# A gated mix of full and local attention: other PSUM banks for the last K block and the first Q, a second DMA queue for the last output rows, and new planner numbers

## The chip, the core and the metric

The kernel runs on one core of one Trainium2 chip. The core has five engines with their own instruction streams: TensorE (PE in the profile; its weight loads are shown apart as PEld), VectorE (DVE), ScalarE (ACT), GpSimd (POOL) and SyncE (SP, which issues nearly all DMAs here). The metric is device time in microseconds, the median of several runs. PSUM, into which TensorE writes, has eight banks of 512 fp32 columns on 128 partitions.

## What is computed

Two attentions over the same 2048 tokens of 640 channels, 32 heads of 20 channels each, mixed by a gate for each token. Branch A is full attention; branch B looks at eight earlier tokens, two apart. In the reference (cut):

```python
def _A_ref(x, wqkv, wo):
    q, k, v = ...                                  # 32 heads of 20
    scores = jnp.einsum("bhqd,bhkd->bhqk", q, k) * scale
    p = _softmax(scores, axis=-1)
    o = jnp.einsum("bhqk,bhkd->bhqd", p, v)
    return merge_heads(o) @ wo

def _B_ref(x, wqkv, wo):
    W, dil = 8, 2
    idx = pos[:, None] - (jnp.arange(W) * dil)[None, :]   # masked where < 0
    ...                                            # softmax over the 8 taps
    return merge_heads(o) @ wo

g = _sigmoid((x * gate_w).sum(-1, keepdims=True))
return g * _A_ref(x, A_wqkv, A_wo) + (1 - g) * _B_ref(x, B_wqkv, B_wo)
```

## The kernel before

**Units and tiles.** Branch A is cut into 32 groups, one for each of 4 query chunks of 512 tokens and 8 quads of heads. A group has 16 K blocks of 128 keys times 4 heads: 64 score blocks of 128 x 512, 2048 in all. TensorE makes a score block as `kT` times `qT` (L1508), an exponential turns it into weights, and TensorE multiplies these by `vA` into the output bank `obank` (L1576). The exponential of most blocks runs on ACT (L1531), two blocks (128x1024) or three (128x1536) to an instruction: a tile. The others "ride": a fourth row group of TensorE makes them into a spare bank, and DVE forms the exponential as an integer that is read as bf16 (L1521, then three shifted copies at L797 that go through `obank` with weighted V). A column of ones in `vA` gives the softmax sum.

**PSUM.** `score[0]` and `score[1]` have three banks each, which alternate from tile to tile; `obank` and `side0` have one each. The third bank of each score tensor, when a tile has only two blocks, serves as a side bank: `side[0]` is `side0`, `side[1]` the third bank of `score[0]`, `side[2]` that of `score[1]`. All other TensorE work (projections, branch B, output projection; L558) and the rides use side banks.

**The order of the work.** The Python code is a list scheduler. `_Sched.task` keeps a modelled time for each engine and appends each task to the stream of its engine; `emit` writes the five streams with semaphores. So the order on each engine is fixed when the program is built. For each tile `s` the main loop issues the score matmuls, the exponential, perhaps a multiplication by V, and then lets other work in (`spend`, `run_side`) until the modelled end of the previous exponential plus a slack. Where modelled TensorE load is below a bound (`FILL`), `filler` (L1597) puts in matmuls whose result is not used. `PLAN` (L50 to L102) sets 18 numbers of these rules anew at certain tiles: slacks, priorities, due times, the bound of the filler, when a DVE ride may open.

**The head** (L1287 to L1345) stands before that loop, in an order written out by hand. x arrives in four chunks, `turn` transposes each into a score tensor (chunks 0 and 2 into `score[0]`, 1 and 3 into `score[1]`; 1280 fp32 columns, so into the third bank too), and `x_out` copies it to `xT` on ACT and DVE. `k_first(0)` to `k_first(3)` project the K of the first head quad, 512 keys each, alternating between `side0` and `obank` (`kbank`, L1252); `k_max` (DVE) takes the largest absolute value in each row, and `k_out` (ACT) copies the block to `kT`. At L1314 the first Q block is projected into `side[1]`. DVE combines the maxima to `KM[0]`, takes |Q| into `qabs[0]`, TensorE adds `KM[0]` times `qabs[0]` to the same bank (L1326; a bound on the scores, which stands in for the row maximum), and DVE scales the bank into `qT[0]` (L1331), which the first scores need. `v_first` and `v_out` make the first V block in `side0`. `bank_free` and `obank_first` tell the scheduler when the banks come free.

**The tail** (L1048 to L1085) makes the last 512 output rows, in four blocks of 128. When the last group's output is normalised (`gen_norm`, DVE), five matmul groups (L1057) add its share; what the other heads and branch B give lies ready in SBUF (`pre`) for blocks 0 and 1, and in two side banks for blocks 2 and 3 (`gen_prefold2`, L1036). ACT copies the first 512 columns of blocks 2 and 3 to `tout` (L1076), DVE adds blocks 0 and 1 (L1079) and the last 128 columns of all four (`tout_r`, L1070). Then SP issues four DMAs of 160 KB each, in the order 0, 1, 2, 3 (L1084).

```python
    kbank = lambda tcc: (side[0], ("side", 0)) if tcc % 2 == 0 else (obank, "obank")   # L1252
...
        for blk in range(4):                                                         # L1082
            row = (QCN - 1) * 512 + blk * P
            T("sp", 2.0, lambda e, blk=blk, row=row: e.dma_start(out_v[row:row + P, :], tout[blk]),
              reads=[("tout", blk), "tout_r"], writes=[("out", row)], dma=True)
```

Of the kernel before, what the change touches and what calls it, by code (L numbers as in the profile page):

```python
# [50 lines left out]
    0: ((0.36, 0.81), 0.32, 2.5, 6.6, 0.49, -1.0, -0.1, 11.8, 7.0, 7.2, 0.52, 0.47, 4.4, 4.44, 0.0, 0.85, 2, 0.0),  # L51
    10: ((0.41, 0.67), 0.29, 2.5, 6.6, 0.49, -1.0, -0.32, 10.6, 6.7, 7.2, 0.52, 0.61, 4.4, 4.44, 0.0, 0.85, 2, 0.0),
    30: ((0.3, 0.64), 0.32, 2.5, 2.5, 0.49, -1.0, -0.1, 11.8, 7.0, 6.95, 0.47, 0.5, 4.97, 4.0, 0.0, 0.85, 2, 0.0),
    40: ((0.42, 0.67), 0.29, 2.5, 6.6, 0.49, -1.0, -0.32, 10.6, 6.7, 7.2, 0.52, 0.61, 4.4, 4.44, 0.0, 0.85, 2, 0),
    70: ((0.41, 0.67), 0.29, 2.5, 2.5, 0.83, -1.02, -0.32, 10.6, 5.5, 7.2, 0.42, 0.61, 5.71, 4.44, -0.04, 0.85, 3, 0.0),
    80: ((0.42, 0.67), 0.29, 5.5, 6.6, 0.49, -1.0, -0.32, 10.6, 6.7, 7.2, 0.52, 0.48, 4.4, 4.44, 0.12, 0.85, 2, 0),
    90: ((0.42, 0.67), 0.05, 2.5, 6.6, 0.49, -1.0, -0.32, 10.6, 6.7, 7.2, 0.52, 0.61, 4.4, 4.44, 0.0, 0.6, 2, 0),
    110: ((0.3, 0.64), 0.32, 2.5, 1.0, 0.49, -1.0, -0.1, 11.8, 7.0, 7.2, 0.4, 0.47, 4.77, 3.55, -0.02, 0.85, 2, 0.0),
    120: ((0.3, 0.61), 0.32, 2.5, 6.3, 0.49, -1.0, -0.1, 10.63, 7.0, 7.2, 0.4, 0.56, 4.29, 4.0, 0.0, 0.85, 2, 1),
    130: ((0.3, 0.61), 0.28, 2.5, 6.3, 0.62, -1.0, -0.1, 10.63, 7.0, 7.2, 0.39, 0.56, 4.29, 4.0, 0.0, 0.85, 2, -3),  # L60
    140: ((0.3, 0.61), 0.22, 2.5, 5.5, 0.4, -1.0, 0.01, 9.77, 7.0, 7.2, 0.33, 0.21, 4.29, 4.0, 0.0, 0.85, 2, 0.0),
    150: ((0.3, 0.64), 0.32, 2.5, 2.5, 0.49, -1.0, -0.35, 11.8, 7.0, 7.2, 0.52, 0.47, 4.4, 4.0, 0.1, 0.85, 2, 0.0),
    190: ((0.3, 0.64), 0.32, 1.0, 2.5, 0.49, -1.0, -0.1, 11.8, 7.0, 7.2, 0.55, 0.47, 4.56, 4.0, 0.0, 0.85, 2, 0.0),
    200: ((0.3, 0.64), 0.32, 1.0, 2.5, 0.49, -0.57, 0.17, 11.8, 7.0, 7.2, 0.55, 0.47, 4.56, 4.0, 0.04, 0.85, 2, 0.0),
    210: ((0.3, 0.64), 0.32, 2.5, 2.5, 0.49, 0.26, 0.1, 11.8, 4.5, 11.1, 0.56, 0.32, 4.97, 4.0, -0.25, 0.85, 2, -3),
    230: ((0.3, 0.64), 0.32, 2.5, 2.5, 0.49, 0.05, -0.54, 11.8, 6.7, 11.1, 0.56, 0.47, 5.29, 2.82, -0.48, 0.85, 2, -3),
    240: ((0.3, 0.64), 0.32, 1.0, 6.3, 0.49, -0.85, -0.1, 11.39, 6.7, 11.1, 0.56, 0.27, 4.97, 4.0, -0.25, 0.85, 2, -3),
    260: ((0.3, 0.64), 0.32, 1.0, 6.3, 0.49, -0.34, -0.1, 11.39, 6.7, 10.86, 0.56, 0.27, 4.97, 4.0, 0.08, 0.85, 2, -3),
    290: ((0.3, 0.64), 0.32, 1.0, 6.3, 0.49, -0.34, -0.1, 11.39, 4.5, 10.86, 0.56, 0.27, 4.97, 4.0, 0.08, 0.85, 2, -3),
    300: ((0.3, 0.64), 0.32, 1.0, 6.3, 0.49, -0.34, -0.1, 11.39, 4.5, 10.86, 0.56, 0.27, 6.29, 4.0, 0.05, 0.85, 2, -3),  # L70
    320: ((0.3, 0.64), 0.27, 1.0, 6.3, 0.49, -0.83, -0.1, 11.39, 4.5, 10.86, 0.69, 0.23, 5.37, 4.0, 0.05, 0.61, 2, -3),
    330: ((0.3, 0.64), 0.27, 1.0, 6.3, 0.49, -0.72, -0.1, 11.39, 4.5, 7.69, 0.69, 0.23, 5.37, 4.0, 0.05, 0.61, 2, -3),
    340: ((0.3, 0.64), 0.14, 1.0, 6.3, 0.49, -1.05, 0.17, 11.39, 6.7, 10.63, 0.3, 0.34, 5.37, 4.43, 0.05, 0.61, 2, -3),
    350: ((0.3, 0.64), 0.16, 1.0, 6.3, 0.49, -0.25, -0.1, 8.61, 6.7, 10.86, 0.56, 0.27, 4.97, 4.0, 0.08, 0.85, 2, -3),
    360: ((0.3, 0.64), 0.27, 1.0, 5.5, 0.7, -0.83, -0.1, 12.93, 4.5, 11.67, 0.69, 0.23, 5.37, 4.0, 0.05, 0.61, 2, -3),
    390: ((0.3, 0.64), 0.27, 1.0, 6.3, 0.7, -0.83, -0.1, 12.93, 7.0, 10.86, 0.69, 0.23, 5.37, 4.0, 0.2, 0.61, 2, -3),
    400: ((0.3, 0.64), 0.27, 1.0, 6.3, 0.7, -0.83, -0.1, 12.93, 7.0, 9.69, 0.69, 0.23, 5.37, 1.85, 0.2, 0.6, 2, -3),
    420: ((0.3, 0.64), 0.27, 1.0, 6.3, 0.7, -0.83, -0.07, 12.93, 4.5, 10.86, 0.5, 0.23, 5.37, 4.0, 0.1, 0.61, 2, -3),
    430: ((0.3, 0.64), 0.27, 1.0, 6.3, 0.7, -0.83, -0.07, 12.93, 6.2, 10.86, 0.5, 0.23, 5.37, 4.0, 0.1, 0.61, 2, -3),
    440: ((0.3, 0.64), 0.27, 1.0, 6.3, 0.7, -0.83, -0.07, 12.93, 4.5, 10.86, 0.5, 0.23, 5.64, 4.45, 0.1, 0.75, 2, -3),  # L80
    460: ((0.3, 0.64), 0.27, 1.0, 5.5, 0.8, -0.83, -0.07, 11.24, 4.5, 10.15, 0.5, 0.23, 5.12, 4.0, 0.1, 0.61, 2, -3),
    470: ((0.3, 0.62), 0.27, 1.0, 5.5, 0.8, -0.83, -0.03, 11.24, 4.5, 10.15, 0.5, 0.23, 5.12, 4.0, 0.2, 0.61, 2, 0),
    480: ((0.3, 0.62), 0.27, 1.0, 5.5, 0.8, -0.83, -0.03, 11.24, 4.5, 10.15, 0.5, 0.2, 5.12, 4.0, 0.2, 0.63, 2, 0),
    490: ((0.3, 0.64), 0.27, 1.0, 5.5, 0.16, -1.11, -0.07, 11.24, 4.5, 10.15, 0.5, 0.22, 5.12, 4.0, 0.1, 0.61, 2, -3),
# [1686 lines left out]
```

## Time and profile before

| what | value |
|---|---|
| median of 5 runs | 841.44 us (840.33 to 842.42) |
| the profiled execution, device time | 840.33 us |
| its span, first to last instruction | 838.5 us |
| granted TensorE clock | 0.998 of full |
| ACT busy, share of the span | 808.3 us, 96% |
| DVE busy | 675.8 us, 81% |
| DMA | 29.16 MB, 35 GB/s on average |

The span is 1.8 us shorter than the device time of the same execution; what lies around it is launch and end. The five runs lie within 2.1 us, and the profiled one is the fastest of them. ACT, DVE and TensorE are all busy for most of the span, so the share of busy time alone doesn't tell which of them sets the end; the order of waits does. A row "xN" of the timeline merges N like instructions, and its second number is the time from the start of the first to the end of the last.

### The profile page before, as it was taken

The page shows a single profiled execution, that of the slowest core. Times are in us where ns is not written, and L with a number is a line of the kernel's source. Part 1 is how long each engine was busy: PE and PEld are TensorE (multiplying, and loading weights), DVE is VectorE, ACT ScalarE, POOL GpSimd, SP SyncE. Part 2 cuts the span into 40 slices and gives each one's busy share as a digit, 9 for nine tenths or more (in the row PEclk, how much of TensorE's full clock was granted, in tenths as well). Part 3 has the DMA queues.
Part 4 walks back from the last instruction along what each step waited for, and adds up shares of the span by engine and source line. Part 5 has one row for each costly group of instructions (what it writes and reads, how often), then busy time and mean ns, then how long its engine had stood idle before and what let it go on. Part 6 is the DMA issues. An engine that isn't in the chain of part 4 may idle for free.

```text
span 838.5 us, 29878 instructions
## 1 busy us (share of the span) xinstructions
PE 790.9 (94%) x12795; PEld 293.3 (35%) x12798; DVE 675.8 (81%) x1183; ACT 808.3 (96%) x747; POOL 129.7 (15%) x177
## 2 busy tenths in 40 slices
PE   8999999999999999999998898999899999999997
PEld 4332322333334333433333333333342333342223
DVE  7577787779887888787888888898898878888763
ACT  4999999999999999999999999999999999999994
POOL 5040111620110110111110111111011111102100
PEclk9999999999999999999999999999999999999999
DMA  9002121200111101010101111010010010100000
GB/s 312 30 19 46 41 45 34 70 16 18 33 29 39 28 20 23 16 32 25 26 18 26 35 20 36 12 42 23 25 32 21 22 34 22 30 7 25 18 5 34
DMA packets 45016, 29.16 MB, mean 35 GB/s; under 512 B 27204, under 2 KB 43684, under 8 KB 44884
## 3 DMA queue, kind: packets, MB, share of 16 engines
q1 hardware_dynamic: 44884, 27.25, 12.5%
q8 instruction: 101, 1.65, 0.8%
q14 instruction: 31, 0.25, 0.1%
HBM read 11.94 MB, written 2.62 MB: 17 GB/s over the span
## 4 chain that ended last, share of the span: by engine, by line
PE 43%; ACT 39%; issue 12%; DVE 4%; SPq 1%; DMA 0%; DVEq 0%; ACTq 0%
ACT ebuf L1531 39%; PE score L1508 13%; PE side L558 10%; PE obank L1576 10%; PE score L558 5%; PE obank L1597 2%; DVE uD L1521 1%; DVE eD L797 1%; PE score L1597 1%; SPq L705 1%; PE side L1597 1%; PE obank L461 1%; PE score L1224 1%; ACT eB L914 0%; PE side L885 0%
## 5 line engine op out<-in xcount | busy, mean ns | idle before, releaser
L1531 ACT ACTIVATE ebuf<-score 128x1024 bf16<-128x1024 f32 (+1 forms) x715 | 797.0, 1261 | 9.7 <-PE score L1508 7.7
L1508 PE MATMUL score<-qT,kT 32*128 32x512 bf16 x2048 | 284.4, 384 | 31.0 <-ACT ebuf L1531 22.5
L1521 DVE TENSOR_SCALAR uD<-score 128x512 int16<-128x512 f32 x311 | 210.1, 685 | 55.9 <-PE score L1508 52.3
L1508 PEld LDWEIGHTS score<-qT,kT 32*128 32x128 bf16 x2048 | 72.0, 91 | 272.7 <-ACT ebuf L1531 125.2
L797 DVE TENSOR_SCALAR eD<-uD 128x2048 int16<-128x2048 int16 (+1 forms) x234 | 161.2, 712 | 3.8 <-PE obank L1576 2.5
L1576 PE MATMUL obank<-ebuf,vA 128*21 128x512 bf16 x1737 | 159.0, 385 | 2.8 <-ACT ebuf L1531 1.4
L558 PE MATMUL side<-xT,kvw 128*32 128x256 bf16 (+1 forms) x2580 | 106.0, 282 | 2.4 <-DVE dst L662 0.9
L789 POOL TENSOR_TENSOR vS<-vA,vw 128x252 bf16<-128x252 bf16 x78 | 53.3, 688 | 275.0 <-PE obank L1576 234.4
L1576 PE MATMUL obank<-eD,vS 128*21 128x512 bf16 x933 | 81.8, 379 | 0.0
L558 PEld LDWEIGHTS side<-xT,kvw 128*32 128x32 bf16 x2580 | 60.7, 96 | 37.5 <-issue 19.9
L765 POOL TENSOR_TENSOR rcp<-rcp,gA 128x16 f32<-128x16 f32 x31 | 9.8, 315 | 368.3 <-DVE rcp L763 368.3
L1576 PEld LDWEIGHTS obank<-ebuf,vA 128*21 128x21 bf16 x1737 | 37.6, 89 | 83.2 <-issue 69.7
L970 DVE TENSOR_TENSOR stage<-qkvB,repB 128x1280 bf16<-128x1280 bf16 x64 | 52.3, 841 | 0.1
L853 DVE CAST qkvB<-side 128x512 bf16<-128x512 f32 (+1 forms) x72 | 42.2, 595 | 11.3 <-PE side L558 10.7
L869 DVE TENSOR_TENSOR stage<-qkvB 128x1280 bf16<-128x1280 bf16 x64 | 50.5, 827 | 0.2
L558 PE MATMUL side<-stage,ident 128*32 128x512 bf16 (+1 forms) x768 | 49.1, 346 | 0.7 <-DVE dst L662 0.5
L1597 PE MATMUL obank<-xT,zero 128*32 128x512 bf16 x560 | 43.6, 382 | 0.0
L770 POOL TENSOR_TENSOR oN<-oTt,rcp 128x512 bf16<-128x512 f32 x31 | 32.5, 1048 | 2.4
L759 DVE STREAM_TRANSPOSE oTt<-obank 128x512 f32<-128x512 f32 x32 | 22.8, 712 | 11.1 <-PE obank L1576 11.0
L1576 PE MATMUL obank<-uD,vA 128*21 128x512 bf16 x311 | 30.3, 379 | 0.0
L772 DVE STREAM_TRANSPOSE oN<-oN 128x512 bf16<-128x512 bf16 x32 | 22.6, 705 | 9.3 <-POOL oN L770 9.0
L1576 PEld LDWEIGHTS obank<-eD,vS 128*21 128x21 bf16 x933 | 23.0, 91 | 15.8 <-issue 2.3
(161 smaller groups left out, 575.5 us busy)
## 6 DMA issues: line engine op xcount, KB each, us to landing
repB<-eB SPq DMA_DIRECT2D x128, 32.0 KB
WqP<-in_A_wqkv_dram SPq DMA_DIRECT2D x16, 160.0 KB
stage<-in_B_wqkv_dram SPq DMA_DIRECT2D x1, 2400.0 KB
oTd<-oN SPq DMA_DIRECT2D x108, 20.0 KB
qT<-dst SPq DMA_DIRECT2D x104, 20.0 KB
out_dram<-outsb SPq DMA_DIRECT2D x12, 160.0 KB
kvw<-in_A_wqkv_dram SPq DMA_DIRECT2D x2, 800.0 KB
oTd<-in_A_x_dram SPq DMA_DIRECT2D x2, 640.0 KB
```

The source lines that it names most:

```text
L558: ins = e.matmul(o[j:k, :], l[:, j:k], r, start=(first and i == 0), stop=(last and i == n - 1), skip_group_check=True)
L770: T(en, c2, lambda e: e.tensor_tensor(oo, ii, ib, ALU.mult), reads=["rcp", "oTt"], writes=["oN0"])
L789: T("pool", 0.7, lambda e: e.tensor_tensor(vS[:, d % 2, :, :], _ap(vA, (kb * NQ + q) * 4 * DV, [[0, K - 1], [1, 4 * DV]]), _ap(vw, 0, [[1, ...
L797: T("dve", 0.11 + 0.1334 * n, lambda e, k=k, sl=sl: e.tensor_scalar(eD[:, sl % NS, 0:512 * n].bitcast(I16), uD[d % 2][:, 0:512 * n].bitcas ...
L853: t = TB(dvc(n * TOK), lambda e, o=o, i=i: e.tensor_copy(o, i), reads=[("side", b)], writes=[key])
L869: TB(dvc(CN * TOK, 2), lambda e, w=w, ks=ks: e.tensor_tensor(prodB(w), qB[:, :, :], ks, ALU.mult), reads=["qB", "kB"], writes=[("prod", w) ...
L970: TB(dvc(CN * TOK, 2), lambda e, w=w, vs=vs, rr=rr: e.tensor_tensor(prodB(w), vs, rr, ALU.mult), reads=["vB", ("repB", w4 % NR)], writes=[ ...
L1508: ins = e.matmul(o, kT[32 * j:32 * j + 32, q, kb * P:(kb + 1) * P], qT[g % NQT][32 * j:32 * j + 32, :], start=True, stop=True)
L1521: t = T("dve", 0.69, lambda e: e.tensor_scalar(uD[d % 2][:, 512 * i:512 * (i + 1)].bitcast(I16), side[x], UOFF, 0.0, op0=ALU.add, op1=ALU. ...
L1531: exps[s] = T("act", actc(512 * n), lambda e: e.activation(ebuf[s % NE][:, 0:512 * n], score[s % 2][:, 0:512 * n], ACTF.Exp, scale=LN2 / S ...
L1576: ins = e.matmul(obank[32 * j:32 * j + DV, :], v, src, start=(kb == 0), stop=(last and k >= len(lst) - 4), skip_group_check=True)
L1597: ins = e.matmul(o[32 * j:32 * j + 32, :], w[:, 32 * j:32 * j + 32] if best else w[:, :], xT[:, 0, 0:512], start=bool(best), stop=bool(bes ...
```

## The change

Four edits:

- The head's last K block (`k_first(3)`) is projected into `side[1]`, the third bank of `score[0]`, in place of `obank`, and the first Q block into `obank` in place of `side[1]`. What reads these banks (`k_max`, `k_out`, |Q|, the bound's matmul, the scaling to `qT[0]`) follows.
- The times at which the scheduler takes the banks as free follow too: `side[1]` and `side[2]` after `k_out(3)`, `obank` after the scaling to `qT[0]`.
- The last four output DMAs are issued in the order 2, 3, 0, 1: blocks 2 and 3 from ACT's queue, blocks 0 and 1 from SP's.
- All rows of `PLAN` are replaced: 46 rows in place of 51, at other tiles and with other numbers. The rules that read them stay.

```diff
 PLAN = {
-    0: ((0.36, 0.81), 0.32, 2.5, 6.6, 0.49, -1.0, -0.1, 11.8, 7.0, 7.2, 0.52, 0.47, 4.4, 4.44, 0.0, 0.85, 2, 0.0),
-    10: ((0.41, 0.67), 0.29, 2.5, 6.6, 0.49, -1.0, -0.32, 10.6, 6.7, 7.2, 0.52, 0.61, 4.4, 4.44, 0.0, 0.85, 2, 0.0),
...
-    320: ((0.3, 0.64), 0.27, 1.0, 6.3, 0.49, -0.83, -0.1, 11.39, 4.5, 10.86, 0.69, 0.23, 5.37, 4.0, 0.05, 0.61, 2, -3),
...
+    0: ((0.3, 0.64), 0.32, 2.5, 2.5, 0.49, -1.0, -0.16, 11.8, 7.0, 8.62, 0.51, 0.47, 4.21, 4.0, 0.0, 0.85, 2, 0.0),
+    8: ((0.25, 0.64), 0.27, 2.5, 2.5, 0.49, -1.0, -0.27, 12.76, 7.0, 7.2, 0.52, 0.47, 4.4, 4.0, 0.0, 0.85, 3, 0.0),
...
+    232: ((0.34, 0.66), 0.37, 2.5, 2.5, 1.29, -1.0, -0.1, 11.8, 5.5, 6.1, 0.5, 0.54, 4.4, 3.8, 0.0, 0.71, 1, -3),
...
 }
@@ tail
-        for blk in range(4):
+        for blk in (2, 3, 0, 1):
             row = (QCN - 1) * 512 + blk * P
-            T("sp", 2.0, lambda e, blk=blk, row=row: e.dma_start(out_v[row:row + P, :], tout[blk]),
+            T("act" if blk > 1 else "sp", 2.0, lambda e, blk=blk, row=row: e.dma_start(out_v[row:row + P, :], tout[blk]),
               reads=[("tout", blk), "tout_r"], writes=[("out", row)], dma=True)
@@ head
-    kbank = lambda tcc: (side[0], ("side", 0)) if tcc % 2 == 0 else (obank, "obank")
+    kbank = lambda tcc: ((side[0], ("side", 0)), (obank, "obank"), (side[0], ("side", 0)), (side[1], ("side", 1)))[tcc]
...
-    T("pe", 1.07, proj5(side[1][:, :], lambda c: WqP[:, c, :], None, 0), reads=WQ + XT(0), writes=[("side", 1)])
+    T("pe", 1.07, proj5(obank[:, :], lambda c: WqP[:, c, :], None, 0), reads=WQ + XT(0), writes=["obank"])
...
-        qabs[0][:, :].bitcast(U16), side[1][:, :].bitcast(U16)[:, 1:1024:2], 0x7FFF, None, op0=ALU.bitwise_and),
-      reads=[("side", 1)], writes=[("qabs", 0)])
-    T("pe", 0.215, lambda e: e.matmul(side[1][:, :], KM[0], qabs[0][:, :], start=False, stop=True, skip_group_check=True),
-      reads=[("KM", 0), ("qabs", 0)], accum=[("side", 1)])
+        qabs[0][:, :].bitcast(U16), obank[:, :].bitcast(U16)[:, 1:1024:2], 0x7FFF, None, op0=ALU.bitwise_and),
+      reads=["obank"], writes=[("qabs", 0)])
+    T("pe", 0.215, lambda e: e.matmul(obank[:, :], KM[0], qabs[0][:, :], start=False, stop=True, skip_group_check=True),
+      reads=[("KM", 0), ("qabs", 0)], accum=["obank"])
     v_first()
     t = k_out(3)
-    obank_first = t.end + LAT["act"]
-    t = T("dve", dvc(512), lambda e: e.tensor_scalar(qT[0][:, :], side[1][:, :], OCT, offs[:, 0:1], op0=ALU.mult, op1=ALU.add),
-          reads=[("side", 1), "offs", ("qTz", 0)], writes=[("qT", 0)])
+    bank_free[1] = bank_free[2] = t.end + LAT["act"]
+    t = T("dve", dvc(512), lambda e: e.tensor_scalar(qT[0][:, :], obank[:, :], OCT, offs[:, 0:1], op0=ALU.mult, op1=ALU.add),
+          reads=["obank", "offs", ("qTz", 0)], writes=[("qT", 0)])
     qkeys[0] = [("qT", 0)]
+    obank_first = t.end + LAT["dve"]
     v_out()
-    bank_free[:] = [t.end + LAT["dve"] + 0.5, t.end + LAT["dve"], t.end + LAT["dve"]]
+    bank_free[0] = t.end + LAT["dve"] + 0.5
```

The scheduler lays its order anew from these numbers. Counted in the two orders: exponentials on ACT 715 before (406 of 128x1024, 308 of 128x1536, one of 128x512) and 722 after (428, 293, 1); rides on DVE 311 and 312; filler matmuls 1008 and 844; the matmuls of projections, branch B and output projection are the same in number.

## The prediction

> **What bounds the kernel now.** I read four views in this order: the groups of instructions with their shapes kept apart, the timeline of the head, that of the end, and the stretches. First the groups and two pieces of ACT's timeline.
>
> ```profile
> L1531 ACT ACTIVATE ebuf<-score 128x1536 bf16<-128x1536 f32 x308 | 432.4, 1504 | 3.8 <-PE score L1508 3.0 <-ACT ebuf L1531 0.3
> L1531 ACT ACTIVATE ebuf<-score 128x1024 bf16<-128x1024 f32 x406 | 398.5, 1078 | 5.8 <-PE score L1508 4.7
> ...
> 31.42 5.61 ACT L1531 ACTIVATE ebuf<-score 128x1024 bf16<-128x1024 f32 x6 [0.29 <-PE score L1508]
> ...
> 657.24 5.49 ACT L1531 ACTIVATE ebuf<-score 128x1536 bf16<-128x1536 f32 x4
> ```
>
> ACT hardly idles before an exponential: 9.6 us in 806 us. But one instruction overlaps the end of the one before, and that hides lost time. Six of 128x1024 take 5.61 us, so start to start (5.61 - 1.08)/5 = 0.906 us; four of 128x1536 (5.49 - 1.50)/3 = 1.33 us. The shortest steps all over the trace are 0.903 and 1.330. At these, with 0.48 for each 128x512 and 0.1 for each gate tile, ACT's work from the first exponential (19.50) to the end of the last (826.17) is 782 us. It took 806.7, so some 25 us are lost where scores come a little late. Three things make the time: a head of 19.5 us, ACT's 782 plus 25, and an end of 12.3.
>
> The two halves of ACT's stretch differ:
>
> ```profile
> 19.50:425.70 406.20, 398.93 (x366) 1.00 0.13 32
> 425.70:821.70 396.00, 393.68 (x347) 1.00 0.09 24
> ```
>
> Each half holds 864 score blocks. At the shortest steps they are 389.2 and 388.4 us of ACT, so the losses are 17.0 and 7.6. I counted what TensorE is given between the score matmuls in the first kernel's order, with 0.216 us for four 512-column matmuls side by side (20 of `obank` take 1.19 us in the chain of waits, with one change of mode), less for narrower ones (0.138, 0.108 and 0.069 for 320, 256 and 128 columns), and 0.11 for each change between row and column mode (a group after a change takes 0.33, without one 0.22): 384.6 and 352.3 us. So TensorE is 4.6 us below ACT in the first half and 36.1 in the second. ACT's loss grows where TensorE has little to spare: 9.4 us of loss for 31.5 us of slack, 0.30 for each.
>
> **Head: the last K block.** The timeline of TensorE, of ACT and of DVE there:
>
> ```profile
> 14.65 1.24 PE L1247 MATMUL obank<-xT,kvw 128*128 128x512 bf16 x5 [0.70 <-ACT kT L1268]
> 15.72 1.24 PE L1247 MATMUL score<-xT,WqP 128*128 128x512 bf16 x5
> 17.75 0.39 PE L1326 MATMUL score<-qabs,eB 128*128 128x512 bf16 x1 [0.79 <-DVE qabs L1323]
> 17.98 0.84 PE L1274 MATMUL side<-kvw,xT 128*128 128x320 bf16 x5
> 19.07 0.39 PE L1508 MATMUL score<-qT,kT 32*128 32x512 bf16 x3 [0.24 <-DVE qT L1331]
> ...
> 13.82 0.68 ACT L1268 ACTIVATE kT<-obank,onesrow 128x512 bf16<-128x512 f32 x1
> ...
> 15.92 0.69 DVE L1261 TENSOR_REDUCE kmx<-obank 128x1 f32<-128x512 f32 x1 [0.72 <-PE obank L1247]
> 16.65 0.35 DVE L1321 SCALAR_TENSOR_TENSOR eB<-eB,kmx 128x128 bf16<-128x128 bf16 x1
> 17.00 0.69 DVE L1323 TENSOR_SCALAR qabs<-score 128x512 uint16<-128x512 uint16 x1
> ```
>
> TensorE waits for ACT's copy of K block 1 out of `obank`, which ends at 14.50; the block starts at 14.65. In `side[1]` nothing is left to wait for: its last reader, the copy of x chunk 2, ended on DVE at 10.71 + 0.96 = 11.67. What is late next is x chunk 3, whose ACT copy ends at 12.90 + 1.02 = 13.92; the K block before ends on TensorE near 13.95. With the 0.12 to 0.15 from an end to the next start, K block 3 starts at 14.07, 0.58 earlier. Q follows 1.07 later, at 15.14, after the copy of 14.50 that now guards it: that wait costs nothing there. Had K block 3 no gain, it would. On DVE the maximum starts at 15.34 (DVE is free at 14.90 + 0.31 = 15.21), and all after it moves by the same 0.58, since each step there is released by the one before. The longer life of Q in `obank` holds up nothing: the next writer of `obank` in both orders is a filler, at 20.76 before, and Q is read by 18.4. The new K block is read by ACT near 16.8, before the first scores at 18.5. No load bounds this: V's and K's weights are issued by 8.5 us and the head doesn't wait for them. The head gives 0.58; bounds 0 (if DVE's chain hung on something else) and 0.70 (all of the wait).
>
> **Tail.** The end of the run, chain of waits and timeline:
>
> ```profile
> 826.47 0.22 PE obank L1576 x4
> 826.68 0.50 PE side L558 x28
> 827.18 4.76 PE score L558 x80
> 831.95 0.33 PE score L1057 x4
> ...
> 832.53 1.09 ACT L1076 ACTIVATE stage<-score 128x512 bf16<-128x512 f32 x2 [6.36 <-PE score L1057]
> 833.18 0.69 DVE L1079 TENSOR_TENSOR stage<-score,dst 128x512 bf16<-128x512 f32 x1
> 833.78 0.68 DVE L1079 TENSOR_TENSOR stage<-score,qabs 128x512 bf16<-128x512 f32 x1
> 833.90 2.21 SPq L1084 DMA_DIRECT2D out_dram<-stage  x4
> ```
>
> With E for the end of the last exponential (826.17), TensorE starts the tail's matmuls at 831.88 = E + 5.71, while the normalised output is ready on DVE at 829.49. It is TensorE's remaining projection that holds the tail: after the last product with V come 28 matmuls of 128 columns and 80 of 512. In the new order eight of the 80 and the narrow ones stand before that product (while the last exponential runs), and eight PV matmuls in place of four come after E. So E + 0.12 + 0.43 + 72 x 4.76/80 (4.28) + 0.11 for the mode = E + 4.94, a gain of 0.77. The normalised output, 0.22 later than before, is at E + 3.5: still hidden.
>
> Then the DMAs. Blocks 2 and 3 are ready when ACT's copies end, at 833.13 and 833.62, but stand in SP's queue behind block 0 (ready 833.87) and block 1 (834.46). The four issues start at 833.90, 834.49, 834.97 and 835.78; SP then waits until 837.73 for the last to land. New: ACT issues blocks 2 and 3 after its two copies, near 833.70 and 834.2 (nothing is queued behind them on ACT), SP issues 0 and 1 at 833.90 and 834.5. The last issue is 1.3 us earlier. What is late next is the transfer: 0.655 MB at the 350 GB/s of this DMA's busy slices is 1.9 us; first data came 0.87 after the first issue, so from 834.57 to 836.4 or 836.6, against 837.35 before. A DMA issued by ACT is not in the trace; bounds from SP's rows: 1.5 if it costs what SP's does and the final waits overlap, 0.3 if two queues share the engines so badly that only one of the 0.33 to 0.39 us issues is saved. I take 1.1, by the nearest row, SP's own. [...]
>
> Tail together 0.77 + 1.1 = 1.87, bounds 1.0 and 2.3.
>
> **Middle: the new order.** ACT has 22 more narrow and 15 fewer wide exponentials: 22 x 0.903 - 15 x 1.330 = -0.08 us at the shortest steps; rides on DVE (312 for 311, 0.69 each) and the shifted copies (234 for 234) are equal, and DVE is 81% busy. But narrow tiles lose more: their mean step is 0.947 before another exponential, 0.044 above the shortest, that of wide ones 1.353, 0.023 above. 22 x 0.044 - 15 x 0.023 = +0.63.
>
> TensorE's share, counted as above in the new order: 378.0 us against ACT's 389.5 in the first half, 350.2 against 388.9 in the second. Slack is 11.5 and 38.7 in place of 4.6 and 36.1: 9.5 more, at 0.30 a gain of 2.85. Most of it is 41 fillers fewer (164 matmuls, 8.9 us), and a filler stands where TensorE had a gap anyway; without fillers the slack grows by only 1.0, a gain of 0.3. I take the middle, 1.6, since either count is as near. Which of the `PLAN` numbers does what, no row shows.
>
> **Sum.** -0.58 - 1.87 - 0.08 + 0.63 - 1.6 = -3.5 us. The profiled execution took 840.33, so 836.8 for it; it lies 1.1 below the median of 841.44, so the median goes to 837.9.
>
> **Rivals.** (1) The new order is worth more than counts show. For it: 17 us are lost in the first half, where scores wait for TensorE, and only 7.6 in the second with the same kind of work. If the first half gets halfway to the second, the middle gives 4.7 in place of 1.05: 834.3. Against: the first half still has the projections, and its slack stays below 12 us. (2) The middle gives back what the ends gain, +2.4: 841.4. For it: the second half's stretch from 425.7 to 492.6 goes from 8.4 us of slack to 4.5, and the scores' bank serves 12 of the 20 Q projections in place of 6. (3) Slower: DVE empties the side banks inside the score tensors too late. A score matmul then waits, and TensorE takes nothing else meanwhile. The profile has such waits for the rides (28.1 us in 60, up to 0.9 each) and other DVE reads; ACT covers most of them. With 0.5 us uncovered at 12 more places the middle costs 6, and 841.44 - 2.45 + 6 = 845.0. It decides from 8 to 9 such places, above 843.1. Against: DVE's work is equal, and the numbers of matmuls and copies are the same.
>
> That the edit does not do what it says is excluded for the banks and the queue, which stand so in the new order.
>
> **Chances.** A measurement of this kernel tells about 0.2% (1.7 us) from no change. Forecast 0.55 (its part below 839.7), rival 1 0.15, rival 2 with the forecast's weak end 0.18, rival 3 0.12. So faster 0.70, within 0.2% 0.18, slower 0.12. The forecast's own range from the bounds: head 0 to 0.70, tail 1.0 to 2.3, TensorE 0.3 to 2.85 and narrow tiles 0.63 or nothing, so 0.7 to 5.9 of gain, 835.5 to 840.7. With the rivals, leaving out the slower one and the far end of the first: 832.5 to 842.5.
>
> **What would show it.** The first exponential at 18.9 and K block 3 at 14.07, released by x chunk 3; else the head's step is wrong. The tail's first matmul at E + 4.9, the last output issue near 834.5 less the shift, the last landing 1.0 to 1.2 us earlier against the tail's start. ACT's stretch at 805.6 us or so from first exponential to last, with more of the gain in the first half. The forecast is wrong if that stretch is longer than 808 or shorter than 802.

## The result and the profile after

The changed kernel takes 844.51 us (median of 27 runs, 840.31 to 848.92) against 841.44 for the kernel before (47 runs, 840.21 to 843.59): ratio 1.0036, 95% interval 1.0026 to 1.0046. It is slower by 0.36%. The forecast was 837.9, and 844.51 lies outside its range of 835.5 to 840.7. The runs also spread over 8.6 us where those of the kernel before spread over 3.4.

The profiled execution after has a span of 840.7 us and a device time of 842.50; that of before had 838.5 and 840.33. Line numbers in the loop and the tail are lower by 4 or 5 (L1531 is now L1527). The three parts of the span, and ACT's loss as the prediction counts it (start to start of exponentials, beyond the shortest steps 0.903 and 1.330):

| part | before | after | forecast of the difference |
|---|---|---|---|
| head, to the first exponential | 19.50 | 18.88 | -0.58 |
| ACT's stretch, first exponential to the end of the last | 806.66 | 810.52 | -1.05 |
| after the last exponential | 12.36 | 11.28 | -1.87 |
| ACT's loss within the stretch | 24.9 | 28.9 | |

The head's timeline, lines that answer to those of before:

```profile
13.94 1.24 PE L1242 MATMUL score<-xT,kvw 128*128 128x512 bf16 x5
...
15.01 1.24 PE L1242 MATMUL obank<-xT,WqP 128*128 128x512 bf16 x5
15.21 0.69 DVE L1256 TENSOR_REDUCE kmx<-score 128x1 f32<-128x512 f32 x1
...
18.88 1.45 ACT L1527 ACTIVATE ebuf<-score 128x1536 bf16<-128x1536 f32 x1 [2.19 <-PE score L1504]
```

The last K block starts at 13.94, straight after x chunk 3 (forecast 14.07, before 14.65), and the first exponential at 18.88 (18.9). The end, from the same view:

```profile
829.46 0.61 PE L1572 MATMUL obank<-ebuf,vA 128*21 128x512 bf16 x8
...
834.22 0.40 PE L1052 MATMUL score<-outsb,oN 128*128 128x128 bf16 x4
...
835.55 0.85 ACTq L1079 DMA_DIRECT2D out_dram<-stage  x2
...
836.24 0.96 SPq L1079 DMA_DIRECT2D out_dram<-stage  x2
```

The last exponential ends at E = 829.40. The tail's matmuls start at E + 4.82 (forecast 4.94, before 5.71), and the last output issue comes 2.6 us after them; it was 3.9. So in this profile head and tail moved as forecast; only the last landing did not, to which we come back. What went wrong is ACT's stretch, by 4.9 us against the forecast. Its two halves, with the exponentials' busy time:

```profile
18.88:425.70 406.82, 398.84 (x374) 1.00 0.13 33
425.70:829.40 403.70, 398.76 (x349) 1.00 0.09 24
```

Added up over 60 us stretches, the loss up to 420 us is 17.0 (before 16.9), and behind it 12.0 (before 8.0). The groups show the same number of score matmuls and slightly longer idle time of ACT before exponentials: 12.6 us in place of 9.7.

One thing stands in the trace of after that before had nowhere between head and tail: a granted clock of a half. Busy time of each engine in stretches of 3.4 us at the two places (PE, PEld, DVE, ACT, POOL with their numbers of instructions, then the granted clock; the last two numbers are of DMA):

```profile
373.40:376.80 3.40, 3.40 (x77) 1.78 (x78) 2.48 (x6) 3.40 (x4) 0.61 (x1) 1.00 0.29 101
376.80:380.20 3.40, 2.57 (x29) 0.59 (x17) 3.19 (x9) 3.18 (x4) 0.00 (x0) 1.00 0.00 0
380.20:383.60 3.40, 3.38 (x53) 1.14 (x54) 2.29 (x6) 3.28 (x6) 1.83 (x3) 0.51 0.11 29
...
752.30:755.70 3.40, 2.42 (x28) 0.72 (x24) 3.05 (x6) 3.40 (x5) 0.00 (x0) 1.00 0.00 0
755.70:759.10 3.40, 3.35 (x30) 0.77 (x27) 2.03 (x8) 2.96 (x3) 1.84 (x3) 0.50 0.02 5
```

In each case a thin stretch (29 and 28 matmuls, where the one ahead of the first has 77) is followed by one at half clock, 3.41 us long in the trace's record of the clock. In the stretch at 376.8 a score matmul takes 414 ns on average, in the next one 568; a product with V 382 and 600. In both thin stretches branch B's chain of maxima runs on DVE. The timeline at 378 us, where TensorE waits:

```profile
377.72 0.10 PEld L1504 LDWEIGHTS score<-qT,kT 32*128 32x128 bf16 x3 [0.44 <-DVE uD L1517]
...
378.52 0.28 DVE L902 TENSOR_TENSOR repB<-repB 32x256 bf16<-32x256 bf16 x1
378.73 0.67 DVE L1517 TENSOR_SCALAR uD<-score 128x512 int16<-128x512 f32 x1
378.85 0.39 PE L906 MATMUL side<-repB,negRep 32*128 32x512 bf16 x1 [0.42 <-DVE repB L902]
```

No filler stands between. In 28 executions of the changed kernel span and mean granted clock go together (correlation -0.84; a fit gives 511 us for a whole unit of clock, so about 1.04 us for each half-clock window, which lowers the mean by 0.002). That is a correlation; what a window costs is tried below.

### The profile page after: what moved, and what is told of

Read it like the earlier page. It is cut to its first block, busy times and chain, and to the rows that moved or that the text cites. A ratio compares the mean times of both kernels' runs of the same rounds, so it can differ in the third digit from the quotient of the medians.

```text
span 840.7 us, 29615 instructions
## 1 busy us (share of the span) xinstructions
PE 786.1 (94%) x12634; PEld 291.9 (35%) x12637; DVE 674.7 (80%) x1184; ACT 809.3 (96%) x754; POOL 138.1 (16%) x177
## 3 DMA queue, kind: packets, MB, share of 16 engines
q1 hardware_dynamic: 44596, 26.92, 12.4%
## 4 chain that ended last, share of the span: by engine, by line
ACT 48%; PE 36%; issue 13%; DVE 3%; SPq 0%; DMA 0%; DVEq 0%; ACTq 0%
ACT ebuf L1527 47%; PE score L1504 11%; PE obank L1572 8%; PE side L553 8%; PE score L553 4%; PE obank L1593 1%; PE score L1593 1%; PE obank L456 1%; PE score L1219 1%; DVE uD L1517 0%; PE side L880 0%; ACT eB L909 0%; SPq L770 0%; ACT tB L943 0%; DVE eD L792 0%
## 5 line engine op out<-in xcount | busy, mean ns | idle before, releaser
L1527 ACT ACTIVATE ebuf<-score 128x1536 bf16<-128x1536 f32 (+1 forms) x722 | 797.6, 1240 | 12.6 <-PE score L1504 10.5
L792 DVE TENSOR_SCALAR eD<-uD 128x2048 int16<-128x2048 int16 x234 | 162.7, 724 | 10.6 <-PE obank L1572 10.1
L1572 PE MATMUL obank<-ebuf,vA 128*21 128x512 bf16 x1736 | 161.2, 386 | 1.0 <-DVE eD L792 0.5
L784 POOL TENSOR_TENSOR vS<-vA,vw 128x252 bf16<-128x252 bf16 x78 | 59.6, 765 | 338.0 <-PE obank L1572 303.9
L553 PE MATMUL side<-xT,kvw 128*32 128x256 bf16 (+1 forms) x2560 | 103.6, 281 | 1.9 <-DVE qkvB L848 1.0
L760 POOL TENSOR_TENSOR rcp<-rcp,gA 128x16 f32<-128x16 f32 x31 | 11.5, 371 | 317.0 <-DVE rcp L758 317.0
L1593 PE MATMUL obank<-xT,zero 128*32 128x512 bf16 x440 | 37.5, 383 | 0.0
L553 PE MATMUL side<-woA_d,oTd 128*32 128x512 bf16 (+3 forms) x560 | 29.6, 301 | 0.0
```

The lines of the kernel that those rows point to most:

```text
L553: ins = e.matmul(o[j:k, :], l[:, j:k], r, start=(first and i == 0), stop=(last and i == n - 1), skip_group_check=True)
L784: T("pool", 0.7, lambda e: e.tensor_tensor(vS[:, d % 2, :, :], _ap(vA, (kb * NQ + q) * 4 * DV, [[0, K - 1], [1, 4 * DV]]), _ap(vw, 0, [[1, ...
L792: T("dve", 0.11 + 0.1334 * n, lambda e, k=k, sl=sl: e.tensor_scalar(eD[:, sl % NS, 0:512 * n].bitcast(I16), uD[d % 2][:, 0:512 * n].bitcas ...
L1527: exps[s] = T("act", actc(512 * n), lambda e: e.activation(ebuf[s % NE][:, 0:512 * n], score[s % 2][:, 0:512 * n], ACTF.Exp, scale=LN2 / S ...
L1572: ins = e.matmul(obank[32 * j:32 * j + DV, :], v, src, start=(kb == 0), stop=(last and k >= len(lst) - 4), skip_group_check=True)
L1593: ins = e.matmul(o[32 * j:32 * j + 32, :], w[:, 32 * j:32 * j + 32] if best else w[:, :], xT[:, 0, 0:512], start=bool(best), stop=bool(bes ...
```

## The experiments

Two theories at first. C: the clock. The new plan has 164 fillers fewer, TensorE runs thinner, its clock drops, and that costs what head and tail gain. The rivals: T (the head and tail edits don't gain, or cost) and S (the new order simply waits more; the clock is a side effect). Times are medians; the ratio is always to runs of the kernel before on the same chip, with its 95% interval. The kernel before had medians of 841.3 to 842.1 on these chips.

**The parts apart.** The first kernel has all rows of the new plan, with head and tail of before. The second is the kernel before with the head and tail edits and the old plan.

```diff
 PLAN = {                                    # first: before, with only this
-    0: ((0.36, 0.81), 0.32, 2.5, 6.6, ...
+    0: ((0.3, 0.64), 0.32, 2.5, 2.5, ...
...
-    kbank = lambda tcc: ... if tcc % 2 == 0 else (obank, "obank")      # second: before, with
+    kbank = lambda tcc: ((side[0], ("side", 0)), (obank, "obank"), (side[0], ("side", 0)), (side[1], ("side", 1)))[tcc]
...
-        for blk in range(4):
+        for blk in (2, 3, 0, 1):
```

> The first kernel's head and tail with the changed kernel's planner numbers (844 filler matmuls, 428 narrow exponentials, as in the changed kernel). Theory C (the new order leaves TensorE too empty in some 3.4 us windows, its clock is halved for the next one, and each such window costs about 1 us): the loss comes with the planner numbers, so this is slower than the changed kernel by what head and tail gave there, 0.6 + 1.1: about 846 us, with granted clocks between 0.986 and 0.998. Rival T (the two queues or the moved banks cost the time): about 841, as the first kernel.

> The changed kernel's head and tail with the first kernel's planner numbers (1008 filler matmuls). Theory C: faster than the first kernel by the head's 0.6 and the tail's 1.1 to 1.9, about 839.5 us, granted clock 0.998 as before. Rival T: slower than the first kernel, about 844.

Plan alone: 843.30 us, ratio 1.0013 (1.0004 to 1.0022). Edits alone: 839.59, ratio 0.9965 (0.9953 to 0.9977); a second set of runs gave 839.80 and 0.9980 (0.9971 to 0.9989). So the edits gain 2 to 2.5 us in the old order, and T falls. The first missed both expectations: it is slower, but by less than the whole kernel, though the loop's order is the same as in the changed kernel. That stays in mind: gain and loss don't add up.

The head edit and the tail edit each alone, on the old plan (as in the diff above, one of the two):

> The first kernel with the head's two banks exchanged alone; the order after the head is the first kernel's, instruction by instruction. Expected by the forecast: first exponential 0.6 us earlier, 841.4. If the later work took the gain back: 842.0, no change.

> The first kernel with the last four output DMAs in the order 2, 3, 0, 1 on two queues, alone. Both kernels with and without the edits put the tail's share at 2.46 - 0.62 = 1.8 of the gain: 840.2. By the forecast's figure for the DMAs (1.1): 840.9. If two queues gain only the issues: 841.3.

Head alone 841.13, ratio 0.9996 (0.9986 to 1.0007): the forecast's 0.58 us fits in it, and so does nothing. Tail alone 839.94, ratio 0.9980 (0.9972 to 0.9989), 1.7 us with an interval of 0.9 to 2.4. The tail of the kernel with both edits, from its timeline (last exponential ends at 825.73):

```profile
831.44 1.26 PE L1057 MATMUL score<-outsb,oN 128*128 128x128 bf16 x7
...
832.77 0.86 ACTq L1084 DMA_DIRECT2D out_dram<-stage  x2
...
833.45 0.96 SPq L1084 DMA_DIRECT2D out_dram<-stage  x2
```

The span ends 5.29 us after the start of these matmuls; in the kernel before it was 6.65. That is 1.36 us for the two queues, where the forecast took 1.1. Nearly all of it is issue time: the last issue starts 2.6 us after the matmuls in place of 3.9, as in the changed kernel, so the 0.7 us of the expectation's last case (841.3, only the issues; SP's two of 0.39 and 0.33) was too little. The matmuls start at E + 5.71 as before, so the forecast's other 0.77 of the tail belongs to the new order alone.

**More and fewer fillers.** The changed kernel with the filler bound raised everywhere to at least 0.85 and to at least 0.70, and the kernel before without any filler:

```diff
+            FILL = max(FILL, 0.85)          # the changed kernel; in another one 0.70
...
     def filler(...):                        # the kernel before
+        return False
```

> The changed kernel with the filler's bound at 0.85 or more all through (1760 filler matmuls in place of 844; the order shifts with it). Theory C: no window with a halved clock, all runs within 2 us of each other, about 840.5 to 842. Rival S (the new order is itself late, the clock only shows it): 844 or more, and a spread as in the changed kernel.

> The changed kernel with the filler's bound at 0.70 or more (1088 filler matmuls in place of 844, 424 narrow exponentials in place of 428; the order shifts with it). Theory C: granted clock 0.997 or more in nearly all executions, spread under 4 us, median 841 to 842.5. Rival S: 844 to 846, since more fillers only take more of TensorE.

> The first kernel without any filler matmul. Theory C: many windows with a halved clock, granted clock 0.95 to 0.985, 850 us or more, with a wide spread. Rival S (fillers only take TensorE's time): 841 or less, granted clock 0.998.

At 0.85 (1760 fillers) the clock is full (0.998 to 1.0) and the time 860.44, ratio 1.0219 (1.0205 to 1.0233); at 0.70 (1088) the clock 0.997 to 1.0 and the time 852.01, ratio 1.0124 (1.0109 to 1.0139). Without fillers the kernel before takes 904.22, ratio 1.0733 (1.0703 to 1.0764), at a clock of 0.93; its trace has 17 half-clock stretches ahead of the tail, 123 us in all. C's direction for the clock held (without fillers it fell below the stated 0.95), its times for the first two failed by 18 and 10 us; S's "844 or more" held at 0.85, at a full clock. Such an edit isn't clean: the scheduler lays the whole order anew from it, and though the clock was full or nearly so (the profile at 0.70 has one half-clock window) the new orders were 16 and 8 us slower than the changed kernel. These runs show that thin TensorE brings half clock, and not what the two drops of the changed kernel cost.

**The drops taken away, with nothing moved.** 36 matmuls that add zeros are put into four tasks, at the two thin stretches. No order changes on any engine.

```diff
+        more = {332: 8, 334: 8, 656: 8, 658: 12}.get(len(tiles) - 1, 0)
...
+            for k in range(more):
+                j = k % 4
+                ins = e.matmul(obank[32 * j:32 * j + 32, :], zero[:, :], xT[:, 0, 0:512], start=False, stop=False, skip_group_check=True)
```

> The changed kernel in its own order, with 36 more matmuls that add zeros (8 in each of the score-times-value tasks of places 332, 334 and 656, 12 in that of place 658), put where the changed kernel's two half-clock stretches begin (376.8 to 380.2 us with 29 matmuls, 752.3 to 755.7 us with 28). Theory C (the plan's fewer fillers leave stretches in which TensorE is too idle, and the clock is halved after them): the half-clock stretches at 380 and 756 are gone from the profile, the granted clock is 0.996 or more, the median is 841 to 842 us and the spread of the runs is narrower than the 840.3 to 848.9 of the changed kernel. Theory S (the clock is a side effect; the new order by itself loses the 4 us, by waits): the median stays at 843.5 to 844.5 us whether the half-clock stretches vanish or not.

The changed kernel was run twice more, once beside it:

> The changed kernel itself, once more, beside the others of this call. Its order between head and tail is that of the run with the planner numbers alone, so by theory C (loss from windows with a halved clock, whose number differs from execution to execution) it is 843.3 - 2.4 = 841 with few such windows and up to 848 with six; the median of all executions 844 as before, and executions with a lower granted clock are longer by 1 to 1.6 us for each 0.002. Rival S (the new order is late by itself): also at a granted clock of 0.998 it stays above 842.5.

> The changed kernel once more, beside the one with 36 zero matmuls on the same chip. Both theories: 843.5 to 844.5 us, 0.2 to 0.4% slower than before; its runs spread over 5 us or more, and its profile shows half-clock stretches near 380 and 756 us if C holds.

The changed kernel took 843.59 and 843.63, both ratios 1.0027 (1.0013 to 1.0041 and to 1.0042), all runs between 841.1 and 848.1. With the 36 zeros: 842.06, ratio 1.0005 (0.9996 to 1.0013), spread 840.5 to 843.2, clock 0.997 to 1.0. More work for TensorE made the kernel 1.6 us faster by the medians, and the spread 2.7 us in place of 5.8 and 7.0. The same places, first the changed kernel in its third profile, then the one with zeros:

```profile
375.10:378.50 3.40, 3.40 (x77) 1.58 (x67) 2.74 (x5) 3.40 (x4) 0.61 (x1) 1.00 0.29 101
378.50:381.90 3.40, 2.58 (x33) 0.72 (x34) 3.19 (x9) 3.18 (x5) 0.00 (x0) 1.00 0.00 0
381.90:385.30 3.40, 3.00 (x58) 1.02 (x54) 2.30 (x6) 3.40 (x5) 1.84 (x3) 0.50 0.14 39
385.30:388.70 3.40, 3.40 (x41) 1.13 (x33) 1.32 (x3) 1.22 (x2) 0.00 (x0) 0.50 0.17 43
388.70:392.10 3.40, 3.40 (x31) 0.76 (x34) 3.17 (x5) 2.48 (x2) 0.00 (x0) 0.50 0.18 46
392.10:395.50 3.40, 3.40 (x82) 1.93 (x81) 2.42 (x5) 3.09 (x3) 0.00 (x0) 0.99 0.07 16
```

```profile
374.20:377.60 3.40, 3.40 (x86) 1.73 (x77) 2.26 (x6) 3.40 (x4) 0.61 (x1) 1.00 0.29 101
377.60:381.00 3.40, 3.03 (x38) 0.83 (x35) 3.23 (x9) 3.18 (x4) 0.00 (x0) 1.00 0.00 0
381.00:384.40 3.40, 2.85 (x64) 1.06 (x61) 2.26 (x5) 3.40 (x6) 1.40 (x3) 1.00 0.08 21
384.40:387.80 3.40, 3.40 (x68) 1.53 (x64) 3.28 (x7) 3.17 (x5) 0.44 (x1) 1.00 0.17 42
```

Here the drop lasted three windows, 10.2 us, and ACT (fourth pair) was busy 1.22 and 2.48 us of 3.4 in two of them: it stood still for lack of scores. ACT's loss between 360 and 420 us is 2.3 to 2.5 where the place keeps its clock, 2.9 with one half window, 5.8 with three; between 720 and 780 it is 1.4 to 1.7 without, 1.6 to 2.6 with one, 3.1 to 3.2 with three. So 1.6 us of the loss go to C. But S is not dead either: at full clock the kernel is still 2 to 2.5 us above the edits in the old order.

**Less work for TensorE, with nothing moved.** The kernel with edits and old plan, each filler cut from four matmuls of 512 columns to one of 64:

```diff
-            for j in range(4):
-                ins = e.matmul(o[32 * j:32 * j + 32, :], w[...], xT[:, 0, 0:512], ...)
+            ins = e.matmul(o[0:32, 0:64], w[...], xT[:, 0, 0:64], ...)
```

> The kernel with the head and tail of the change in the old order of the loop (839.59 us), every filler cut from four matmuls of 512 columns to one of 64, and nothing moved: all waits between engines stay as they are, TensorE has less to do. The fillers were there for no result, so the output is the same. Theory C: TensorE's emptier stretches bring half-clock windows (at least ten, granted clock below 0.99), and the time is 845 to 900 us though TensorE has less work. Theory S (less work for TensorE is slack, as the forecast counted it: 0.30 us of ScalarE's loss per us of TensorE's slack): not slower than 839.6 us, by its own rate some us faster.

840.75 us, ratio 1.0009 (0.9988 to 1.0030), clock 0.969 to 0.989. Both expectations failed. The half-clock windows came, eight groups of them between 167 and 819 us, but the kernel lost 1.0 us by the medians and 2.4 to 3.7 by the ratios, where C had said at least 5. And S failed in sign: the fillers' 1008 matmuls, some 54 us of TensorE by the forecast's 0.216 for four, were nearly all gone, and the kernel was not faster by the forecast's 0.30 for each (16 us), but slower. In the parts without a half window (0 to 120, 240 to 300, 360 to 420, 540 to 600 and 660 to 780 us) ACT's loss is 13.0 us, against 13.1 in the same parts before. One of the groups:

```profile
515.15:518.56 3.41, 2.00 (x22) 0.64 (x19) 2.89 (x9) 3.41 (x3) 0.59 (x1) 1.00 0.12 30
518.56:521.97 3.41, 3.02 (x25) 0.86 (x25) 2.43 (x5) 3.41 (x5) 0.00 (x0) 0.50 0.09 24
521.97:525.39 3.42, 3.42 (x46) 1.08 (x43) 1.95 (x4) 3.14 (x3) 0.00 (x0) 0.50 0.21 55
```

ACT hardly idles in these two half-clock windows: it is busy 3.41 and 3.14 of 3.4 us, where in two of the changed kernel's it was busy 1.22 and 2.48. So a half-clock window did not take the same from ACT each time; that it depends on how many scores are ready there is the author's reading, and no run varies that.

**The late landing.** In the changed kernel's profiles the tail ends 6.46 us after the start of its matmuls (before 6.65), though the last issue is 1.3 us earlier. In the trace's record of DMA completions, 15 of the 16 of the last output DMA come by E + 9.42 and one at E + 10.57. Its last packet of 4 bytes ended at E + 9.52, just behind an instruction fetch of 8192 bytes (E + 9.20 to 9.51); the others' ended by 9.04. The trace doesn't name a packet's DMA engine; that the packet stood behind the fetch on the same one is read from these times. Nor do the packets explain why this completion comes 1.05 us after its packet, where the others take some 0.4. The end of the run follows the last completion by 0.7 us. The changed kernel with the old order of the last four issues, all from SP:

```diff
-        for blk in (2, 3, 0, 1):
+        for blk in range(4):
...
-            T("act" if blk > 1 else "sp", 2.0, ...
+            T("sp", 2.0, ...
```

> The changed kernel with its last four output rows issued by SyncE alone and in the old order of blocks; everything else as changed. In the old order of the loop the two-queue tail was worth 1.3 to 1.5 us. In the changed kernel's profiles one of the 16 landings of the last output row came 1.1 us after the others, right behind a fetch of instructions. If that late landing is there in every execution, the two queues bring the changed kernel only about 0.2 us, and this kernel takes as long as the changed one beside it, within 0.5 us. If it belongs to the profile alone, this kernel is 1.1 to 1.6 us slower than the changed one beside it.

846.08 us from 6 runs, ratio 1.0052 (1.0034 to 1.0070), 2.5 us above the changed kernel beside it, which speaks for the second reading. The intervals overlap, though, there are six runs, and their mean clock was a little lower (0.993 against 0.994; by the fit 0.5 us), so this settles nothing.

**Four kernels at full clock.** With the zeros at the thin stretches the clock blurs the times less. So on one chip: the edits in the old order; the new order with zeros and the head and tail of before; the changed kernel with zeros; and this one with all four issues from SP. The diffs are those above, combined. Theory A: head and tail bring their gain in either order, and the rest is the new order's. Theory I: part of it is lost in the new order.

> The head and tail of the change in the old order of the loop, again, on the same chip as the next three. Theory A (head and tail bring the forecast's 2.45 us in either order, and the new order costs what is left): 2.0 to 3.0 us below before. Theory I (they bring less than the forecast in the new order): the same here; it is the yardstick.

> Before's head and tail with the new order of the loop, and the 36 matmuls that add zeros at the two places whose emptiness halved the clock: the new order at full clock. Theory A: the new order alone costs 3.0 to 3.5 us at full clock, so 844 to 845 us, 2.0 to 3.0 us above the same order with the new head and tail (842.1 us). Theory I: the new order alone costs about 1 us, 842 to 843 us, within 1.2 us of the kernel with the new head and tail; then something of their gain is lost in the new order. Both: clock 0.997 or more, spread of 3 us at most.

> The changed kernel with the 36 zero matmuls, again, beside the others of this call. Both theories: 841.5 to 842.5 us, clock 0.997 or more, no half-clock stretch at 380 or 756 us.

> As the run before, with the last four output rows issued by SyncE alone in the old order of blocks. Theory A: 1.1 to 1.6 us slower than it, the gain that the two queues had in the old order, so 843.2 to 844.0 us; the late landing of the changed kernel's profile is then the profile's own. Theory I: within 0.5 us of it, 841.6 to 842.6 us: the late landing behind a fetch of instructions takes the two queues' gain away in every execution.

| order of the loop | head and tail | us | ratio | interval |
|---|---|---|---|---|
| old | old | 841.81 | 1 | |
| old | new | 839.80 | 0.9980 | 0.9971 to 0.9989 |
| new, zeros | old | 842.85 | 1.0014 | 1.0006 to 1.0023 |
| new, zeros | new | 841.79 | 1.0002 | 0.9993 to 1.0011 |
| new, zeros | new head, issues from SP | 842.56 | 1.0004 | 0.9995 to 1.0013 |

The third kernel's profile has one half-clock window again, at 761.9 us, so its expectation held for the time and the mean clock and not for the stretch. Head and tail edits bring 2.0 us in the old order and 1.1 in the new; the two queues alone bring 0.8 there by the medians and 0.2 by the ratios, where they brought 1.4 by the old order's profile. Theory I is nearer: 1.1 where A had 2.0 to 3.0, and for the two queues less than A's 1.1. That the fetch is the reason is argued from the traces, and no run moves the fetch: four of five profiles of the new order with two queues have that packet at E + 9.52, behind the fetch, and end at E + 11.26 to 11.28. The fifth (that of the last but one row) has it at E + 9.20, ahead of the fetch; its last completion comes at E + 9.82 and the end at E + 10.53. With SP alone the end is E + 11.72 to 11.80. By these profiles the two queues gain 1.2 us when the fetch comes behind the last packet, 0.5 when it comes ahead of it.

The zeros also suggest that a half-clock window has no fixed price. The plan alone took 843.30 without them (ratio 1.0013, one such window in its profile) and 842.85 with them (1.0014), so by the ratios, each good to 0.0009, no gain; the changed kernel's ratio went from 1.0027 to 1.0005. Nor is the old order free of such windows: the second profile of the edits alone has one, at 605.1 us.

The new order itself, at full clock: +1.0 us (0.5 to 1.9 by the interval of the ratio). Its stretch is 809.4, 809.7 and 809.8 us in three profiles without any half window, against 806.7, 806.9, 807.0 and 808.5 in four of the old order; 2.4 longer on average, of which its shorter tail gives 0.6 back (E + 11.8 in place of 12.4). TensorE's waits (us in total, times, longest), the old order first, the new one with zeros second:

```profile
PEld score L1509 <- DVE uD L1522: 28.1, 60, 0.9
...
PE score L1509 <- ACT ebuf L1532: 22.5, 61, 1.0
...
PE score L1509 <- DVE uD L1522: 0.6, 2, 0.4
```

```profile
PEld score L1504 <- DVE uD L1517: 37.9, 77, 1.1
...
PE score L1504 <- ACT ebuf L1527: 27.3, 65, 1.0
...
PE score L1504 <- DVE uD L1517: 2.8, 8, 0.8
```

Score matmuls wait longer for a free bank: 4.8 us more for ACT's exponential and 2.2 more for DVE's ride; their weight loads (PEld) wait 9.8 us more for DVE's rides, 77 times in place of 60. Waits for ACT are no loss by themselves, since ACT is then busy; waits for DVE may be. An estimate from the traces: take each exponential that starts over 0.05 us later than the shortest step allows, and look whether its scores or their weight loads waited for DVE in the 0.9 us before. In the four profiles of the old order 3.0 to 3.7 us of ACT's loss stand behind such a wait (23 or 24 exponentials), in the three of the new order 6.4 to 6.6 (29 or 30). That is about all by which the new order's loss is larger. It is read from traces; no run takes these waits away. At full clock ACT's loss is 16.8 up to 420 us (before 16.9) and 11.4 behind it (before 8.0). Which rows of the plan do this wasn't tried.

## Why the prediction was wrong

**Head, right in this profile, with a wait that the forecast did not see.** K block 3 at 13.94, first exponential at 18.88: 0.62 in the profile for 0.58. What was named as late next, x chunk 3, is what releases it. But 0.11 of the 0.62 is luck: the second x chunk's transposes start at 7.08 in place of 7.19. From there to the first exponential it is 12.31 us in all five profiles without the head's edit, and with it 11.8 (a gain of 0.5) in eight and 11.9 to 12.2 (0.1 to 0.4) in five. What takes the gain in the five is a small operation on DVE beside a copy on GpSimd; here in the last kernel of the table above (issues from SP):

```profile
12.13 3.99 POOL L1291 COPY kT<-ones 128x1024 f32<-128x1024 f32 x4
...
15.13 1.03 DVE L1313 TENSOR_SCALAR eB<-eB,kmx 128x128 bf16<-128x128 bf16 x1
...
16.08 0.68 DVE L1256 TENSOR_REDUCE kmx<-score 128x1 f32<-128x512 f32 x1
```

The operation ends at 16.16, just after GpSimd's fourth copy (16.12); in the first profile of the changed kernel it starts at 14.83, ends after the third copy and takes 0.41. The forecast had DVE "free at 14.90 + 0.31 = 15.21", as if that time were the operation's own.

**Tail, right in the old order, cut in the new.** The start of the tail's matmuls gained 0.89 (0.77 forecast). The two queues gained 1.36 in the old order (1.1 forecast, bounds 0.3 to 1.5). In the new order the end came only 0.2 earlier against the tail's start in the first profile, and the last landing 0.1; the forecast said 1.0 to 1.2. It asked what is late next after the issues and answered the transfer; by the times of the packets (the fetch to E + 9.51, the last packet to 9.52), an instruction fetch was.

**The middle, wrong, and this is the step that failed.** "41 fillers fewer ..., and a filler stands where TensorE had a gap anyway", and with it the whole term of -1.6 for TensorE's slack (0.30 us of ACT's loss for each), which stands midway between counting the fillers as slack and leaving them out. It failed twice. First as a rate: the two halves of the trace before differ in slack and in loss, but nothing showed that one makes the other. In the new order the first half had 6.9 us more slack by the forecast's own count and lost the same (16.8 for 16.9); with nearly all filler work removed and no order moved, the undisturbed parts lost 13.0 for 13.1. Second, a filler is not worth nothing: where it fills a gap it can keep the clock. 36 matmuls put in at two gaps made the kernel 1.6 us faster. (The term also has a slip: 9.5 us of slack less the fillers' 8.9 is 0.6, not 1.0, which is 0.1 us of time.) Without the term of -1.6 the middle was +0.55, and at full clock the stretch still came out about 2.4 longer. By the estimate above the rest is waits for DVE; ACT's loss grew behind 420 us, where the counts had shown 2.6 us more slack.

**The sum.** From the kernel before, 841.81: the new order at full clock +1.0, head and tail edits -1.1 (in place of -2.0), half-clock windows +1.6 to 1.8 (843.59 and 843.63 without the zeros, 842.06 and 841.79 with them). That makes 843.4 to 843.6; it is put together from these same runs, so it tests nothing. The first measurement, 844.51, is 0.9 above it, with an interval of 2.2 to 3.9 us above before; how many half windows an execution catches differs (two in the first profile, six in the next two). Rival (3) comes nearest. It named score matmuls that wait for DVE, 12 more places of 0.5 us; the row that it quoted, of weight loads, grew from 60 to 77 places, and about 3 us of its 6 showed in ACT's loss. Its sum, 845.0, is 0.5 from the measured 844.51, and that is partly luck: it had neither the clock's 1.6 us nor the edits' lost gain. Rival (2), 841.4, had no mechanism that showed. The forecast's own test, a stretch longer than 808, said that it was wrong: 810.5.

The best kernel of the study is the one with the head and tail edits and the old plan: 839.6 to 839.8 us, ratio 0.9965 and 0.9980.

## What to carry over

Work that produces nothing can be what keeps TensorE's clock (36 zero matmuls here, 1.6 us); before counting its removal as slack, look for the stretches that it fills, and ask what a half clock there costs. A rate between slack and loss taken from two halves of one trace is a correlation: test it by thinning work with the order kept. And price a change of a scheduler's numbers apart from hand-made edits beside it: here the edits gained 2 us with the old numbers, and the new numbers took more. Where the forecast had put a rival's row on record (weight loads that wait for DVE), that row was the one to read first in the new trace.

## What the runs showed of the hardware

- The clock dropped with TensorE never idle for long. Between 25 and 825 us the longest gap of TensorE in the profile after is 0.95 us, and TensorE was busy for 2.42 and 2.57 us of the 3.4 ahead of the two drops (71% and 76%).
- Between head and tail the half-clock stretches of these traces are multiples of 3.41 us and lie on a grid of 3.41 us: the two drops of the profile after (380.24 and 755.70 us) begin 110.0 such windows apart. The grid's phase differs between executions: in the changed kernel's third profile the drop begins at 381.9, half a window later on the grid. The changed kernel lost one window at each place in the first profile and three in the next two, and its 28 mean clocks go from 0.986 to 0.999. That the phase decides this, by catching a thin place whole in one execution and split in another, is the author's reading; no run sets the phase.
- Busy time did not tell which window drops: after the stretch at 759.1 with 2.19 us busy in 3.4 the clock stayed full, after that at 376.8 with 2.57 it fell. Columns streamed did better (counted from the matmul records, of which some are missing): over 18 traces, between head and tail, all full-clock windows below 10,240 columns were followed by half clock, none above 13,312, and some of those between. The median window has 20,500 to 23,000. In the profile after, 10,240 and 10,752 columns stood ahead of the two drops, the window at 759.12 with 11,008 was followed by full clock, and the median is 21,504.
- One completion of an output DMA came late where its last packet ended right behind an instruction fetch: 10.57 us after E where its fifteen fellows came by 9.42, and the run ended 0.7 us later than in the profile where the packet went ahead of the fetch. It is so in four of five profiles; that the fetch is the cause is read from these times alone.
- A VectorE operation on 128x128 took 0.31 to 1.03 us and ended 0.05 us after one of GpSimd's copies beside it, in all 18 traces (L1313 and its like in the other kernels): 15.20 after 15.15 in the profile before, 15.24 after 15.19 in that of after.
